# First block of a gated attention kernel: gates in two loads, a reciprocal on VectorE, split hat product, new order of issue

## The chip, the core and the metric

The kernel runs on one core of a Trainium2 chip. A core has a tensor engine (PE, with its weight loads PEld), a vector engine (DVE), a scalar engine for functions by table (ACT), a general engine (POOL) and a sync engine (SP) that mostly issues DMAs; ACT can issue DMAs too, on a queue of its own. Each engine works through its own instructions in the order in which they are written and waits on semaphores for the others. The metric is device time in microseconds of one execution; lower is better.

## The reference

Two stages follow each other. The first is a linear attention with complex gates, over batch 4, 8 heads, 768 tokens and head size 48:

```python
mag = np.sqrt(a_re * a_re + a_im * a_im)
scale = np.minimum(mag, 0.999) / (mag + 1e-06)
a_re_n, a_im_n = (a_re * scale, a_im * scale)
...
for t in range(S):
    new_re = ar * S_re - ai * S_im
    new_im = ar * S_im + ai * S_re
    S_re, S_im = (new_re + kv, new_im)
    y[:, :, t] = np.einsum('bhd,bhde->bhe', q[:, :, t], S_re)
```

`ar`, `ai` are the gates of token t, and `kv` the outer product of its key and value. The second stage is a soft mixture of experts over the 3072 tokens: slot logits, a softmax over tokens that forms 32 slot inputs, eight experts of two layers, and a softmax over slots that combines their outputs.

## The kernel before

The 768 tokens of a batch are 6 blocks of 128; the 4 batches make 24 blocks, each with the 384 values (8 heads of 48) of a token along the free dimension. Three blocks are one unit (u), loaded together: gates into `aat` (real and imaginary part), q and k into `qkt`, values into `vt`, each tile in two buffers. The first unit is loaded in pieces by `load_first`, the first block's pieces by themselves.

The recurrence is turned into products. `gates` makes from a gate its log magnitude and its tangent: Ln of the real part, the reciprocal of the real part as the exponential of minus that Ln, imaginary part times reciprocal, the square with a running maximum, Ln(1 + square), and three more steps that clip the magnitude. Its steps alternate between ACT and DVE. `arctan` gives the phase. `expo` sums log magnitudes over the tokens of a block by one product with a triangle of ones (L731) and takes exp(+) and exp(-) on ACT (L738, L740); the last row of it, the block's decay, goes to DRAM (`rows`, L743) and comes back transposed as `rt` (`decay`, L747). `phase` sums phases in the same way (L696, L700), rounds them (L704) and makes sine and cosine (L714, L719). `mults` multiplies q and k by the exponentials (L754) and then both by cosine and sine into `hat` (L759). `xpose` turns `hat` on PE (L771) and copies it out (`hT`), `score` multiplies and masks (L782, L786), `attend` gives the block's output, and `delta` carries the state on: the product of k's `hat` and v (L820), the sum with the state before (L825) and the decay from `rt` (L827). `xform`, `logits`, `slots` and `shares` feed the second stage, whose expert products come at the end.

Everything runs in an order written by hand as a list, `ORDER`. Each name in it is a task, and each time that it occurs the task goes on by one step; `_InOrder.pin` fixes each engine's sequence to the list. Steps of different engines do not wait for each other because of the list, only because of data or buffers. The names that matter here: `i` a piece of the first loads; `L` and `T` the two loads of ACT's function table; `g0` the gates of the first block, `g1` those of the other two of the first unit, `g2` on those of later units; `t` the arctangent; `e`, `p`, `m` `expo`, `phase` and `mults` of a block; `x` an `xpose` (four a block; odd numbers are k, even ones q), `c` a score, `a` the output, `D` the state; `la`, `lq`, `lv` the loads of a later unit; `d` the return of the decay rows of a unit; `gl` and `rp` smaller loads on SP; `wu` one of 19 filler products on PE with a tile of zeros (L937), whose result nothing reads; `w` a load of expert weights.

The first unit's gates go through `gates` twice, as group 0 (block 0) and group 1 (blocks 1 and 2); the other groups are whole units. In group 0 the working tiles are 128 by 384, in group 1 128 by 768, from group 2 on 128 by 1152.

Of the kernel before, what the change touches and what calls it, by code (L numbers as in the profile page):

```python
# [310 lines left out]


ORDER = """
    i0 wu17 L0 wu5 wu1 g0 g0 g0 g0 g0 g0 g0 i3 g0 i4 g1 g1 i1 tr0 i2 g1 wu7 g1 wu6 la0 e0 e0 e0 wu18 wu9 wu14 T0 t0 e0 m0 p0 p0
    t1 wu13 p0 p0 p0 p0 L1 p1 p1 p1 wu8 m0 rp1 rp1 g1 g1 g1 p2 wu15 wu16 i6 p1 x3 g1 x3 wu10 p2 p2 p2 x2 g2 x2 g2 g2 i7 e1 wu3
    e1 wu4 e2 e2 e2 wu12 gl0 x0 e1 x1 c1 D0 g2 g2 D0 m1 T1 lq0 rp0 t2 x0 x1 c0 p1 p1 wu11 c1 p1 p2 gl1 p2 p2 g2 gl2 p3 p3 L2 g2
    la1 c0 a0 a0 a0 m1 m2 x5 x5 p3 x7 g2 x7 wu2 x4 x4 wu0 p3 m2 e1 e2 d0 D0 i8 g3 g3 g3 g3 e3 e3 e3 m3 e3 e5 e5 x6 e5 x10 x10
    x11 p4 x11 p4 p4 e4 p4 D1 g3 g3 c2 D1 D1 p5 e4 e4 lv0 p5 x6 x8 x9 c3 g3 c2 T2 p3 p3 p3 x8 x9 g3 t3 a1 c3 a1 a1 m3 e4 p5 p4
    p4 D2 D2 m4 p4 p5 p6 D1 p5 p5 c4 D2 D2 p6 c4 p5 x13 p6 la2 c5 x13 e5 d1 c5 m5 D3 x12 g4 a2 rp0 a2 m4 x12 c6 c6 L3 p7 a2 l0
    l0 l0 g4 e6 x19 g4 g4 lq1 e6 x16 e6 x16 e8 p7 e8 e8 g4 p7 p7 p8 x19 D3 D3 lv1 x14 m6 x14 f2 f2 g4 g4 e7 e7 e7 x15 x15 f0 x18  # L320
    x18 x17 x17 q0 q0 q0 f0 D4 D3 g4 p8 s0 m5 p8 e6 D4 q0 c7 c7 c9 la3 x21 T3 e7 t4 x21 g4 a3 a3 w0 x20 s0 c8 p6 p8 p6 c9 p6 q0
    x23 a3 p9 s0 q0 x22 x20 p9 x23 g5 e8 d2 c8 a4 a4 D4 x22 m6 D5 x27 x26 p7 p7 p7 lq2 p8 p8 p8 q0 x27 c10 m7 p9 m7 p9 a4 x26
    e10 p9 c11 L4 g5 c10 x24 x24 g5 f1 f1 p10 e9 e10 e10 D5 x25 x25 c11 D4 a5 a5 x31 x31 m8 m8 g5 e9 g5 e9 e9 c13 c13 a5 g5 x29
    s0 c12 D5 c12 x28 p10 p10 p10 e11 p11 e11 lq3 e11 x29 g5 p9 x28 x33 x33 m9 a6 a6 a6 l1 x30 l1 g5 x30 p11 p11 T4 g5 p11 c14
    c14 D6 m11 D6 D6 p9 x32 x32 p11 p11 l1 f4 f4 x34 t5 q1 x34 D6 c15 p10 f3 p10 p10 x35 p11 x35 f3 D7 D7 la4 p12 c15 e10 a7 g6
    lv2 a7 a7 m9 x36 x36 c16 q1 L5 m10 m10 c16 D7 D7 w1 c17 c17 p12 x37 p12 x37 g6 s0 q1 a8 c18 s0 p13 c18 g6 g6 g5 q1 g6 x41
    x41 p13 p13 p13 g5 a8 a8 x38 x38 x43 x43 x39 x39 D8 p14 q1 e11 s1 d3 x42 x42 x40 q1 q1 g6 g6 a9 e12 e12 e12 f5 e14 e14 e14
    D8 D8 x40 m11 e13 e13 e13 c19 c19 f5 lv3 g6 c21 m12 p14 p14 c20 T5 x45 x45 f6 f6 a9 la5 p14 D9 c21 t6 s1 x46 D9 e12 g6 a9
    p12 p12 p12 p13 g6 c20 x44 s1 p15 D8 p13 p13 f7 D9 f7 p14 p15 p15 x46 x44 x47 x47 e13 l2 a10 a10 m12 x51 x51 w2 g6 g7 p15
    p16 l2 c22 m13 p15 p15 p15 x48 x48 c22 x50 x50 m13 p14 D9 D10 m14 D10 p16 a10 p16 p16 s1 x49 x49 c23 q2 x52 c25 p14 L6 e15  # L330
    c24 e15 g7 e15 q2 q2 e16 m14 g7 a11 c23 a11 e14 d4 a11 D10 D11 x52 c25 p17 l2 s2 x56 g7 c24 g7 e16 e17 x53 x53 e17 e17 D11
    e16 q2 D11 x54 x55 x55 a12 g7 a12 x56 x54 a12 l3 l3 g7 s1 x57 lq4 x57 x58 g7 x58 s1 p17 T6 D12 c26 D12 m15 m15 p17 c27 q2 f8
    c28 t7 p16 p16 c26 p16 q2 c27 e15 p17 p17 f8 x59 x59 g7 q2 e16 x60 p18 p18 a13 gl0 m16 p18 p18 p18 e17 c28 a13 a13 p19 x60
    c29 p17 s2 s2 lq5 p17 la6 g7 p18 D11 x61 f10 lv4 c29 D12 D12 i5 s2 s2 a14 a14 g7 m16 x61 L7 g8 c30 s2 f10 p19 D13 D13 g8 x67
    lv5 x67 d5 c30 p19 x63 x63 x62 q3 x62 f11 f11 x64 m17 m17 x64 D13 f9 x66 w3 a14 x65 x65 p19 p20 c31 c31 q3 g8 l3 f9 a15 a15
    x66 gl1 e18 e18 e18 c32 s3 a15 q3 g8 g8 g8 e20 e20 c33 c33 e20 D14 e19 D14 x70 e18 f12 e19 l4 x70 e19 T7 t8 e19 f12 e20 D13
    c32 a16 q3 a16 a16 m18 x71 x69 x71 x69 m18 x72 x73 g8 l4 p20 w4 x72 p20 x68 x68 p19 D14 D15 D14 p19 p19 m19 x73 p20 p21 D15
    p20 s3 s3 p20 p20 c35 m19 c35 L8 c34 c34 s3 c36 q4 q3 q3 q3 l4 x75 q4 g8 g8 x74 x74 x75 a17 a17 a17 c36 s3 s3 w5 l5 l5 x76
    g8 g8 s4 x76 x77 x77 c37 d6 f13 c37 gl2 e22 e22 e22 m20 p21 m20 a18 a18 x78 f13 c38 p21 l5 D15 f14 x78 lv6 q4 q4 f14 p21 p22
    x79 e23 e23 e23 D16 q4 D16 c38 q4 q4 D16 x80 x80 p22 p22 p22 p23 e21 f15 f15 D17 x79 q5 e21 q5 e21 T8 D16 p21 p21 x82 D17  # L340
    c39 x81 f16 a18 s4 x81 lq6 e21 e22 p21 p23 x82 a19 c39 m22 a19 a19 f16 s4 s4 m21 m21 s4 f17 f17 p22 p23 c40 x83 D17 D18 c40
    x86 p23 x83 p23 p22 x86 x87 x87 p22 s4 c41 c41 a20 p23 p23 a20 x85 D17 x85 L9 x84 x84 f18 w6 w7 a20 D18 w8 m22 x91 x91 m23
    m23 q5 q5 c43 c43 l6 f18 x90 c42 x94 x93 x93 q5 q5 x94 x90 c42 a21 a21 c45 a21 e23 d7 D18 D18 D19 l6 l6 c45 x89 x89 x88 q5
    D19 x88 x92 x92 x95 x95 c44 D19 c44 f20 c46 s5 s5 D19 q6 q6 a22 a22 s6 s5 q6 q6 q6 a22 c46 c47 a23 f20 c47 a23 q6 q6 s5 s5
    s5 a23 l7 w9 f19 f19 w10 l7 l7 s6 s6 s6 q7 q7 f23 me0 me0 f21 q7 q7 s7 s6 s6 f23 ze0 f22 f21 f22 s7 w13 er4 s7 s7 me0 me0
    me0 me0 s7 s7 me0 er4 me0 er0 er1 q7 er1 q7 er0 si0 si0 w12 w11 G0 er2 H0 H0 H0 H0 q7 H0 H0 H0 H0 H0 H0 R0 U0 er2 er7 er8 H0
    er7 U0 U0 H0 R1 X0 X0 X0 X1 X1 er6 U1 X0 X0 X0 G0 U1 U1 X0 X0 X0 X1 X1 er8 er6 X0 X0 X0 X0 X0 X0 w14 w15 G0 G0 X0 O0 O0 X1
    X1 X1 X1 X1 w16 w17 w18 A0 A2 A2 er5 A1 A1 A0 X1 X1 X1 X1 X2 X1 X1 X1 O1 A4 er3 er5 A5 A4 A6 S0 A5 A6 S2 X2 X2 X2 X2 X2 er3
    A3 A3 O1 A8 A8 A7 A7 S3 A9 A10 X2 A9 X2 X2 X2 X2 X2 S1 G0 X2 X2 X2 X2 O2 A11 A11 A10 S5 S4 A12 G0 A13 O2 A14 A12 A13 S6 A15
    A15 A19 A19 A18 A14 S8 A18 S11 S7 A16 A16 A20 A20 S10 A17 A17 S9 G0  # L350
"""


# [192 lines left out]
def _polar(ctx, tc, cst, phi_sb, rp, bad, aa, qk, vv, phi, w1, w2, consts, out):  # L546

    nc = tc.nc
    PE, ACT, DVE, POOL, SP = nc.tensor, nc.scalar, nc.vector, nc.gpsimd, nc.sync
# [51 lines left out]
    def load_first(x):
        if x in (0, 3, 4) and 0 not in aat:
            aat[0] = io.tile([P, UB, 2, HD], F32, name="aat")
        if x in (2, 7) and 0 not in qkt:
# [15 lines left out]
        SP.dma_start(out=o, in_=i)  # L620
# [14 lines left out]
    def gates(x):  # L635
        u, j0, j1 = GROUPS[x]
        ar, ai = aat[u][:, j0:j1, 0], aat[u][:, j0:j1, 1]
        if u not in tmp:
# [5 lines left out]
        ACT.activation(out=ar, in_=ar, func=AF.Ln)
# [1 line left out]
        ACT.activation(out=t, in_=ar, func=AF.Exp, scale=-1.0)  # L646
# [1 line left out]
        DVE.tensor_tensor(out=ai, in0=ai, in1=t, op=ALU.mult)  # L648
# [102 lines left out]
    def mults(g):  # L751
        u, j = divmod(g, UB)
        qk = qkt[u][:, j]
        DVE.tensor_tensor(out=qk, in0=ee[g], in1=qk, op=ALU.mult)  # L754
# [4 lines left out]
        DVE.tensor_tensor(  # L759
            out=x,  # L760
            in0=qk.rearrange("p w (h d) -> p w h d", d=D).unsqueeze(3).broadcast_to(sh),
            in1=cs[g].unsqueeze(1).broadcast_to(sh),
            op=ALU.mult,
        )
# [358 lines left out]
```

## Time and profile before

| | us |
|---|---|
| three runs | 285.72, 286.18, 286.17 |
| median | 286.17 |
| the profiled execution | 285.81 |
| its span, first to last instruction | 283.8 |

All durations here come from one profiled execution, whose span is the time from its first to its last instruction. A row of the order in time gives the start, the duration, the engine, the line of the kernel, the operation, what it writes and reads, the shapes, how many instructions the row merges, and in brackets how long the engine was idle before it and what ended that. An engine's name with a q behind it is its sequencer, which issues DMAs. A row of the stretches gives the length of the stretch and each engine's busy time in it. A row of a tile gives the least, middle and largest duration in ns. Busy time of PE includes the fillers, and starts of neighbouring instructions on one engine can overlap a little.

### The profile page before, as it was taken

The numbers are of one execution on the slowest core, as the hardware profiler recorded it, in microseconds if no ns is written. First come the engines' busy times: TensorE is split into PE (matmuls) and PEld (weight loads), VectorE is DVE, ScalarE is ACT, GpSimd is POOL, SyncE is SP. The second block draws the span as 40 slices with busy tenths as digits, with TensorE's granted clock in tenths as the row PEclk, the third lists the DMA queues.
The fourth block names the chain that finished last, engine by engine and source line by source line (L and its number), as shares of the span: only waits on it lengthen the run. The fifth ranks groups of instructions, "written<-read, shape, count | busy, mean of one in ns | idle before, by whom it ended". The sixth has DMA issues, their size and how long they took to land.

```text
span 283.8 us, 6886 instructions
## 1 busy us (share of the span) xinstructions
PE 272.3 (96%) x2835; PEld 216.4 (76%) x2835; DVE 227.9 (80%) x411; ACT 220.9 (78%) x398; POOL 4.9 (2%) x11
## 2 busy tenths in 40 slices
PE   8999999999999999999999999999999999999970
PEld 3347658979888987989989799988888996438650
DVE  2689998999999999999999999999779566523550
ACT  4776999999999999999999999988886454111250
POOL 0200000000000000000000000000000002000000
PEclk9999999999999999999999999999999999999997
DMA  7996236453653962092457550884068599998395
GB/s 253 392 321 222 66 24 142 155 197 105 212 170 21 338 209 50 38 270 56 163 27 266 181 188 1 60 311 182 3 112 334 193 425 416 420 419 355 126 366 191
DMA packets 21398, 56.61 MB, mean 200 GB/s; under 512 B 11696, under 2 KB 13552, under 8 KB 16496
## 3 DMA queue, kind: packets, MB, share of 16 engines
q1 hardware_dynamic: 20968, 56.10, 59.7%
q8 instruction: 24, 0.39, 0.6%
q14 instruction: 14, 0.11, 0.1%
q10 hardware_dynamic: 392, 0.00, 0.1%
HBM read 51.34 MB, written 4.76 MB: 198 GB/s over the span
## 4 chain that ended last, share of the span: by engine, by line


## 5 line engine op out<-in xcount | busy, mean ns | idle before, releaser
L777 ACT COPY hT<-tp 96x512 f32<-96x512 f32 x92 | 51.2, 588 | 7.3 <-PE tp L771 6.9
L771 PE MATMUL tp<-cst,hat 128*96 128x128 f32 x384 | 53.7, 274 | 0.0
L782 PE MATMUL sp<-hT,hT 96*128 96x128 f32 x384 | 50.9, 278 | 0.0
L782 PEld LDWEIGHTS sp<-hT,hT 96*128 96x128 f32 x384 | 46.9, 192 | 2.0 <-issue 0.7
L771 PEld LDWEIGHTS tp<-cst,hat 128*96 128x96 f32 x384 | 41.8, 128 | 8.3 <-issue 5.2
L759 DVE TENSOR_TENSOR hat<-qkt,cs 128x1536 f32<-128x1536 f32 x24 | 42.0, 1750 | 1.2 <-PE tp L771 0.4
L786 DVE TENSOR_TENSOR scT<-sp,cst 128x512 f32<-128x512 f32 x48 | 32.6, 684 | 6.9 <-PE sp L782 6.8
L807 PE MATMUL yb<-scT,vt 128*48 128x128 f32 x384 | 36.2, 277 | 0.0
L820 PEld LDWEIGHTS db<-vt,hat 128*96 128x96 f32 x320 | 31.0, 165 | 2.5 <-issue 1.5
L820 PE MATMUL db<-vt,hat 128*96 128x48 f32 x320 | 31.5, 245 | 0.0
L809 PE MATMUL yb<-hT,st 96*48 96x128 f32 x320 | 31.1, 272 | 0.0
L807 PEld LDWEIGHTS yb<-scT,vt 128*48 128x48 f32 x384 | 20.7, 122 | 8.1 <-issue 5.1
L754 DVE TENSOR_TENSOR qkt<-ee,qkt 128x768 f32<-128x768 f32 x24 | 22.7, 946 | 0.4 <-ACT ee L740 0.4
L937 PE MATMUL wp<-xs 128*128 128x512 f32 x38 | 21.3, 682 | 1.0 <-POOL xs L932 1.0
L696 PE MATMUL up<-aat,cst 128*128 128x384 f32 x48 | 20.0, 498 | 0.5 <-ACT ee L740 0.2
L809 PEld LDWEIGHTS yb<-hT,st 96*48 96x48 f32 x320 | 19.1, 123 | 0.0
L812 ACT COPY yT<-yb 128x512 f32<-128x512 f32 x24 | 14.2, 591 | 4.8 <-PE yb L809 4.7
L719 ACT ACTIVATE cs<-n,kb 128x384 f32<-128x384 f32 x24 | 14.6, 613 | 0.7 <-DVE n L717 0.7
L648 DVE TENSOR_TENSOR aat<-aat,gt 128x1152 f32<-128x1152 f32 (+2 forms) x9 | 11.0, 1222 | 4.9 <-ACT gt L646 4.9
L832 PE MATMUL xp<-cst,yT 128*128 128x128 f32 x96 | 14.5, 274 | 0.0
L937 PEld LDWEIGHTS wp<-xs 128*128 128x128 f32 x38 | 7.8, 220 | 8.5 <-issue 5.3
L709 DVE SCALAR_TENSOR_TENSOR f<-n,up 128x384 f32<-128x384 f32 x24 | 13.1, 547 | 1.5 <-ACT n L706 1.4
(147 smaller groups left out, 448.3 us busy)
## 6 DMA issues: line engine op xcount, KB each, us to landing
wx<-in_w_dram SPq DMA_DIRECT2D x13, 1024.0 KB
aat<-in_aa_dram SPq DMA_DIRECT2D x7, 1152.0 KB
qkt<-in_qk_dram SPq DMA_DIRECT2D x7, 1152.0 KB
we<-in_w_dram SPq DMA_DIRECT2D x5, 1024.0 KB
vt<-in_vv_dram SPq DMA_DIRECT2D x8, 576.0 KB
aat<-in_w_dram SPq DMA_DIRECT2D x2, 1024.0 KB
qkt<-in_w_dram SPq DMA_DIRECT2D x2, 1024.0 KB
wt<-in_w_dram SPq DMA_DIRECT2D x2, 1024.0 KB
```

Of the source, the lines that this page charges most:

```text
L696: PE.matmul(out=up, lhsT=tri_u[par], rhs=ph, start=True, stop=not by_pe)
L719: ACT.activation(out=t[:, :, 0, :], in_=a.rearrange("p (h d) -> p h d", d=D), func=AF.Sin, scale=-TWO_PI, bias=kb[:, 2:3])
L754: DVE.tensor_tensor(out=qk, in0=ee[g], in1=qk, op=ALU.mult)
L759: DVE.tensor_tensor(out=x, in0=qk.rearrange("p w (h d) -> p w h d", d=D).unsqueeze(3).broadcast_to(sh), in1=cs[g].unsqueeze(1).broadcast_t ...
L771: PE.transpose(out=tp[:, a, :], in_=hat[g][w][:, 4 * hh + a].rearrange("p c d -> p (c d)"), identity=ident)
L777: ACT.copy(out=hT[g, hh, w], in_=tp)
L782: PE.matmul(out=sp[:, a, :], lhsT=hT[g, hh, 1][:, a, :], rhs=hT[g, hh, 0][:, a, :], start=True, stop=True)
L786: DVE.tensor_tensor(out=t, in0=sp, in1=mask[g % 2].unsqueeze(1).broadcast_to([P, 4, P]), op=ALU.mult)
L807: PE.matmul(out=o, lhsT=vt[u][:, j, h, :], rhs=scT[g, hh][:, a, :], start=True, stop=first)
L809: PE.matmul(out=o, lhsT=st[g - 1][:, h, :], rhs=hT[g, hh, 0][:, a, :], start=False, stop=True)
L820: PE.matmul(out=db[:, h, :], lhsT=hat[g][1][:, h].rearrange("p c d -> p (c d)"), rhs=vt[u][:, j, h, :], start=True, stop=True)
L937: PE.matmul(out=wp.rearrange("p (a c) -> p a c", a=4), lhsT=blank, rhs=blank.unsqueeze(1).broadcast_to([P, 4, P]), start=True, stop=True)
```

## The change

Five things change, the first four in the first unit alone.

1. The gates of block 0 come in two loads instead of one: the real part on SP's queue (`i0`), the imaginary part as a new piece `i9`, issued by ACT ahead of its first table load.
2. In group 0 DVE's `reciprocal` takes the place of ACT's exponential of minus Ln. Ln is still needed; it writes over the real part, and comes behind the reciprocal.
3. `mults` of block 0 makes `hat` in two instructions, k's half and then q's, instead of one.
4. The loads of the first unit are issued in another order: the gates of block 2 before those of block 1, and q and k of blocks 1 and 2 (`i7`) before those of block 0 (`i2`).
5. `ORDER` is a new list, over the whole length of the kernel, of the same tasks: other positions of products, copies, loads and fillers on every engine.

On DVE the new list begins with the first block's steps as before; then the two halves of `hat` stand in front of p1's rounding, and D0's multiply with the decay stands in front of m2's `hat`. On PE four fillers instead of five stand in front of e0's product, three behind it as before, and the q transpose x2 stands ahead of the k transpose x3. On SP the sequence begins (list names):

```
before: i0 i3 i4 i1 i2 la1 rp1 i6 i7 gl0 lq1 rp0 gl1 gl2 la2 e1 e2 d0 d0 i8 ...
after:  i0 i4 i3 i1 i7 i2 rp1 la1 i6 i8 e1 la2 e2 d0 d0 lq1 gl1 lq2 la3 lv1 ...
```

The diff, with the list cut to its first lines:

```diff
 ORDER = """
-    i0 wu17 L0 wu5 wu1 g0 g0 g0 g0 g0 g0 g0 i3 g0 i4 g1 g1 i1 tr0 i2 g1 wu7 g1 wu6 la0 e0 e0 e0 wu18 wu9 wu14 T0 t0 e0 m0 p0 p0
-    t1 wu13 p0 p0 p0 p0 L1 p1 p1 p1 wu8 m0 rp1 rp1 g1 g1 g1 p2 wu15 wu16 i6 p1 x3 g1 x3 wu10 p2 p2 p2 x2 g2 x2 g2 g2 i7 e1 wu3
...
+    i9 wu0 wu11 wu4 i0 g0 L0 i4 g0 g0 g0 g0 g0 g0 g0 i3 g1 g1 g1 i1 wu1 e0 e0 e0 i7 i2 wu2 wu12 g1 T0 wu16 tr0 t0 p0 rp1 e0 m0
+    wu10 t1 p1 p0 p0 p1 p0 p0 p0 m0 m0 wu5 L1 p1 g1 g1 p2 wu8 p1 x2 x2 wu9 g1 g1 la0 x3 x3 p2 p2 wu6 p2 x1 x1 e2 g2 g2 i6 D0 g2
...
@@ load_first
-        if x in (0, 3, 4) and 0 not in aat:
+        if x in (0, 3, 4, 9) and 0 not in aat:
...
-            lambda: (aat[0][:, 0:1], aa[0][:, 0:1]),
+            lambda: (aat[0][:, 0:1, 0], aa[0][:, 0:1, 0]),
...
+            lambda: (aat[0][:, 0:1, 1], aa[0][:, 0:1, 1]),
         )[x]()
-        SP.dma_start(out=o, in_=i)
+        (ACT if x == 9 else SP).dma_start(out=o, in_=i)
@@ gates
+        if x < 1:
+            DVE.reciprocal(out=t, in_=ar)
+            yield "g2"
         ACT.activation(out=ar, in_=ar, func=AF.Ln)
-        yield "g2"
-        ACT.activation(out=t, in_=ar, func=AF.Exp, scale=-1.0)
+        if x >= 1:
+            yield "g2"
+            ACT.activation(out=t, in_=ar, func=AF.Exp, scale=-1.0)
         yield "g3"
@@ mults
-        sh = [P, 2, H, 2, D]
-        DVE.tensor_tensor(
-            out=x,
-            in0=qk.rearrange("p w (h d) -> p w h d", d=D).unsqueeze(3).broadcast_to(sh),
-            in1=cs[g].unsqueeze(1).broadcast_to(sh),
-            op=ALU.mult,
-        )
+        for w in (slice(0, 2),) if g else (slice(1, 2), slice(0, 1)):
+            sh = [P, w.stop - w.start, H, 2, D]
+            DVE.tensor_tensor(
+                out=x[:, w],
+                in0=qk[:, w].rearrange("p w (h d) -> p w h d", d=D).unsqueeze(3).broadcast_to(sh),
+                in1=cs[g].unsqueeze(1).broadcast_to(sh),
+                op=ALU.mult,
+            )
+            if w.start:
+                yield "m1"
-    for x in range(9):
+    for x in range(10):
         at("i", load_first, x)
```

More of the change, by code (lines that the diff above doesn't have):

```diff
@@ L322 @@
[L322 to L325, printed above, removed]
@@ new lines @@
+    g3 D1 c2 gl1 lq1 c2 p5 p5 x9 e5 e5 la2 g3 p5 m3 g3 D2 T2 p3 p5 c3 p3 p3 p5 p5 p5 lv0 x10 x10 c3 x11 g3 gl2 m3 t3 rp0 wu13 a1
+    a1 x11 c4 D1 D2 a1 x13 p6 p4 p4 p4 x12 x13 x12 c5 e6 p6 D2 D3 e3 e4 m5 L3 e5 c4 a2 d1 c5 a2 g4 a2 p6 c6 g4 l0 e6 e6 D3 m4 m4
+    D2 e6 g4 x14 x14 p7 p7 l0 c6 p7 l0 s0 x15 x15 D3 g4 g4 p7 x19 x19 e7 e7 e7 x18 x18 D4 D4 g4 f0 f0 x17 m5 e8 e8 e8 q0 q0 q0
+    x16 x16 c7 x17 p8 g4 p8 p8 f2 g4 c7 m6 x23 T3 i5 e7 p6 rp0 f2 p6 p6 p8 x23 c8 a3 q0 c9 q0 m8 q0 a3 a3 x22 c8 x22 t4 x21 x21
@@ new lines @@
+    x20 s0 D3 a4 c9 a4 c11 x20 c10 p8 p8 p8 m6 g4 lv1 x24 D4 a4 la3 q0 g5 D5 p7 D5 p7 p7 L4 g5 gl0 s0 x24 p9 p9 p9 D4 e9 f1 m7
+    f1 g5 c11 c10 w0 e9 e9 a5 a5 m7 x26 e8 d2 D5 D6 x28 x27 x26 a5 lq2 x27 p9 p10 p10 p10 e10 lv2 g5 x28 e10 e10 g5 g5 x25 p10
+    x30 x30 D6 l1 x31 x25 m8 e11 x31 l1 q1 e11 e11 c13 g5 g5 q1 q1 lq3 x29 c12 x29 T4 t5 p11 p9 p9 c13 m10 f3 p11 c12 c14 a6 a6
+    x33 p11 f3 p9 D6 D7 a6 q1 D6 p10 m9 c14 p11 p11 p10 p10 p11 x32 x32 c15 c15 p11 a7 a7 la4 m9 g5 D7 D7 x33 L5 p12 p12 x34 a7
@@ new lines @@
+    p12 D7 x34 s0 c16 e9 e10 c16 m11 q1 q1 g5 x37 x37 x35 x35 s0 s0 q1 g6 a8 e11 D8 d3 g5 x36 x36 D8 c17 g6 l1 s1 m10 e12 g6 e12
+    e12 e12 x39 x39 c17 e14 e14 e14 x38 x38 x40 c18 p13 x40 g6 a8 c18 x41 x41 p13 p13 x43 x43 s1 x42 D8 g6 p13 p14 s1 g6 g6 c19
+    c19 f4 f4 a8 p14 p14 e13 f6 e13 x42 f6 e13 g6 T5 p12 p12 D8 D9 p14 D9 m11 c21 t6 a9 a9 m12 c20 a9 e13 p13 p12 m14 f5 c21 f5
+    l2 x47 x47 la5 x46 e14 c20 x45 x46 D9 p15 p14 g6 x45 p15 p14 p14 lv3 f7 f7 p13 x44 x44 l2 c23 q2 d4 m12 a10 a10 p13 D9 p15
```

54 lines of the change are left out of this document (23 added, 31 removed).

## The prediction

> **What bounds the kernel now.** I read the page first, then the engines' busy time by stretch, then the first 20 us in order of time. The chain of waits that ended last is empty in this trace, so the bound has to be read from who idles where. Engines and, below them, stretches (busy us of PE, its weight loads, DVE, ACT, POOL; granted clock; DMA share; GB/s):
>
> ```profile
> span 283.8 us, 6886 instructions
> PE 272.3 (96%) x2835; PEld 216.4 (76%) x2835; DVE 227.9 (80%) x411; ACT 220.9 (78%) x398; POOL 4.9 (2%) x11
> ```
>
> ```profile
> 0.00:5.00 5.00, 4.01 (x5) 1.85 (x6) 0.66 (x6) 2.12 (x3) 0.41 (x5) 1.00 0.63 217
> 5.00:10.00 5.00, 4.56 (x9) 1.73 (x8) 2.31 (x6) 3.12 (x6) 0.48 (x1) 1.00 1.02 388
> 60.00:80.00 20.00, 20.00 (x197) 17.66 (x196) 19.53 (x32) 19.90 (x40) 0.00 (x0) 1.00 0.42 133
> 160.00:180.00 20.00, 20.00 (x233) 18.48 (x230) 18.89 (x30) 19.85 (x37) 0.00 (x0) 1.00 0.35 88
> 200.00:220.00 20.00, 20.00 (x222) 17.67 (x221) 16.14 (x29) 15.74 (x30) 0.00 (x0) 1.00 0.53 159
> ```
>
> In 60 to 180 ACT is never free (19.9 of 20 us) and DVE hardly (18.9 to 19.5): this middle moves only if it starts earlier or has less to do. From 200 PE has no gap while the others have some. In the first 10 us ACT works 5.2 and DVE 3.0 us, and PE mostly runs the filler products of L937: this stage is latency, one block's gates in a single file. A microsecond gained or lost there moves the start of a full pipeline, and I carry it to the end unless something absorbs it. The file itself:
>
> ```profile
> 4.13 0.52 ACT L644 ACTIVATE aat<-aat 128x384 f32<-128x384 f32 x1 [2.11 <-DMA aat<-in_aa_dram]
> 4.68 0.52 ACT L646 ACTIVATE gt<-aat 128x384 f32<-128x384 f32 x1
> 5.24 0.56 DVE L648 TENSOR_TENSOR aat<-aat,gt 128x384 f32<-128x384 f32 x1 [3.67 <-ACT gt L646]
> 5.83 0.56 DVE L650 CUSTOM_DVE_ANT_0 gt<-aat 128x384 f32<-128x384 f32 x1
> 6.43 0.62 ACT L652 ACTIVATE gt<-gt,kb 128x384 f32<-128x384 f32 x1 [1.23 <-DVE tmax L650]
> 8.32 0.56 DVE L658 SCALAR_TENSOR_TENSOR aat<-aat,gt 128x384 f32<-128x384 f32 x1 [0.68 <-ACT gt L656]
> 8.93 0.91 PE L731 MATMUL lp<-aat,cst 128*128 128x384 f32 x2 [0.44 <-DVE aat L658]
> 9.88 0.49 ACT L738 ACTIVATE ee<-lp 128x384 f32<-128x384 f32 x1
> ```
>
> Gates land at 4.13; Ln and the exponential end at 5.20; the multiply starts at 5.24; each following step starts 0.04 to 0.05 us after the one before it, up to the first product at 8.93.
>
> **The reciprocal.** It replaces the exponential (0.52 us) and takes Ln out of the file: the multiply now waits for the reciprocal alone. Ln writes over the reciprocal's input, so it starts after it, but beside the multiply and the square (5.24 to 6.39 before), whose 1.15 us hide its 0.52. No reciprocal of 384 elements is in the trace; of its kind there are 3 elements and 1:
>
> ```profile
> L150 DVE TENSOR_SCALAR csum<-csum x8: 168/169/169, 69.5 to 239.1; 128x3 f32<-128x3 f32 x8
> L151 DVE RECIPROCAL csum<-csum x8: 175/176/177, 69.7 to 239.3; 128x3 f32<-128x3 f32 x8
> L131 DVE TENSOR_SCALAR nm<-m x1: 150/150/150, 60.0 to 60.0; 96x1 f32<-96x1 f32 x1
> L220 DVE RECIPROCAL rz<-rz x1: 158/158/158, 242.2 to 242.2; 96x1 f32<-96x1 f32 x1
> 9.93 0.96 DVE L648 TENSOR_TENSOR aat<-aat,gt 128x768 f32<-128x768 f32 x1 [1.05 <-ACT gt L646]
> 41.26 0.95 DVE L754 TENSOR_TENSOR qkt<-ee,qkt 128x768 f32<-128x768 f32 x1
> ```
>
> An ordinary DVE operation pays (0.96 - 0.56) / 384 = 1.04 ns an element. **Lower end**: the reciprocal does too, 0.56 us. **Upper end**: the line through its own two rows, (176 - 158) / 2 = 9 ns an element, 0.158 + 383 x 0.009 = 3.6 us. TENSOR_SCALAR makes the same step from 1 to 3 (150 to 169), so the step alone proves nothing. But the reciprocal's own rows are the nearest there are, and I take them, with the smallest slope that they allow, (175 - 158) / 2 = 8.5 ns: **3.4 us**. [...]
>
> **Two loads, two queues.** Before:
>
> ```profile
> 0.73 1.34 SPq L620 DMA_DIRECT2D aat<-in_aa_dram  x3
> 0.73 1.28 ACT L580 ACT_TABLE_LOAD   x1 [0.73 <-PEq L1100]
> 10.40 1.23 ACTq L743 DMA_DIRECT2D rows<-ee  x1
> ```
>
> The real parts, half of the bytes, now come first; the imaginary ones go out on ACT's queue beside them. If a half lands sooner by its share of the transfer, 192 KB at 388 GB/s = 0.5 us, the reciprocal starts at 3.65; if both halves share the engines it starts at 4.1, as before. I take 3.9. [...] Issuing on ACT stands ahead of the table load: SP's three take 1.34 us, 0.45 each; ACT's only one takes 1.23. The load then ends at 2.5 to 3.3, still before 3.9: hidden. Without that cover Ln would pay, which nothing waits for before 8 us.
>
> Sum of the gates: reciprocal 3.9 to 7.3, multiply at 7.33 instead of 5.24: **+2.1 us** (with 0.56 us: multiply at 4.5, -0.75). The first product, ACT's two exponentials, the table load behind them and the phase follow at the same distance; first-block work on ACT is one file, so nothing else fills it. At +2.1 the other loads are not late: the first block's q and k, now behind the 768 KB of the other two, have, by the tiles' shapes, 192 + 192 + 768 + 320 + 768 + 384 KB = 2.69 MB to wait for; 5 x 217 + 5 x 388 GB/s is 3.0 MB by 10 us, against a use after the exponentials of 9.88.
>
> **k ahead of q.** Before, p1's rounding stood in front of the hat product:
>
> ```profile
> 15.20 0.60 ACT L719 ACTIVATE cs<-n,kb 128x384 f32<-128x384 f32 x1
> 15.93 0.56 DVE L704 TENSOR_SCALAR n<-up 128x384 f32<-128x384 f32 x1 [0.80 <-PE up L700]
> 16.41 1.75 DVE L759 TENSOR_TENSOR hat<-qkt,cs 128x1536 f32<-128x1536 f32 x1
> 18.08 0.96 DVE L654 SCALAR_TENSOR_TENSOR aat<-aat,gt 128x768 f32<-128x768 f32 x1
> ```
>
> Now the two halves come right after the cosine and the rounding after them. Each half is L754's form, 0.95 us, and such rows start 0.08 us before the end of the one before: 1.82 for both instead of 1.75, 0.07 more. They save about 0.6 of waiting for the rounding and hand it to the rounding. The new order gives PE a q transpose first (x2 ahead of x3), so k's earlier half serves only the state product D0. Net for the gate of the next blocks (L654, behind both in either order): 0.
>
> **A wait that the new order adds.** DVE's first state multiply (L827) needs the last decay row, which goes through DRAM and back:
>
> ```profile
> 25.06 0.33 SPq L591 DMA_DIRECT2D aat<-in_aa_dram  x1
> 25.50 1.56 SPq L743 DMA_DIRECT2D rows<-ee  x2
> 35.15 0.81 SPq L747 DMA_DIRECT2D rt<-rows  x2
> 36.17 1.75 DVE L759 TENSOR_TENSOR hat<-qkt,cs 128x1536 f32<-128x1536 f32 x1
> 37.84 0.55 DVE L827 TENSOR_TENSOR st<-db,rt 96x384 f32<-96x384 f32 x1
> ```
>
> Rows left at 25.50 to 27.06 and were back only after 35.96. The multiply stood behind m2's hat (36.17 to 37.92) and needn't have waited. It now stands ahead of that hat, so it comes due some 1.75 us earlier in its engine; one of the two rows now goes ahead of the 1152 KB gate load, which brings the return forward by up to about 1 us. The wait is between 0 and 1.75 us; I take 0.9 on DVE, with m2's hat, the next gates and through them ACT queued behind it. ACT has other blocks' work ready, so I count half: +0.4. The same order puts block 3's q and k (lq1) behind that return on SP, and the other loads that share its queue; their users come after 41 us, so 0, between 0 and 1 if the rows come back late. DVE's idle time elsewhere (0.5 to 1.1 of 20 us in the middle) gives 0.4 back.
>
> The rest of the new order is the same set of operations, 19 fillers included; its effect is bounded by ACT's and DVE's idle time in one stretch, 0.1 to 1.1 us, either way, and I take 0.
>
> **Sum**: 2.1 + 0.4 - 0.4 = +2.1 on the profiled execution's 285.81 (283.8 of span and 2.0 around it): 287.9. That execution lies 0.36 below the median of the three runs, so the median should read **288.2**.
>
> **Rivals.**
>
> *The reciprocal at one element a cycle* (ends on the other side). Price 0.56 us; then the multiply starts at 4.5, q's half of the hat ends at 16.9 instead of 18.16, and the next gate's L654 starts about 0.7 us earlier, less 0.4 for the state multiply's wait: -0.5 with a range of -1.3 to +0.3, 285.7 in the median. It decides as soon as the reciprocal costs less than what it replaces with the time won at landing, 5.20 - 3.9 = 1.3 us. For it: the ordinary slope and TENSOR_SCALAR's equal step. Against: its own two rows.
>
> *The clock falls too.* At the end PE's clock dropped once PE had stopped:
>
> ```profile
> 274.48 0.86 PE L301 MATMUL o<-er,sr 128*128 128x512 f32 x3 [0.34 <-ACT os L307]
> 276.60:280.00 3.40, 0.00 (x0) 0.00 (x0) 0.00 (x0) 0.00 (x0) 0.00 (x0) 1.00 0.99 353
> 280.10:283.80 3.70, 0.00 (x0) 0.00 (x0) 0.00 (x0) 0.00 (x0) 0.00 (x0) 0.50 0.11 40
> 0.99 7.50 PE L937 MATMUL wp<-xs 128*128 128x512 f32 x10 [0.99 <-POOL xs L932]
> 13.39 1.02 PE L937 MATMUL wp<-xs 128*128 128x512 f32 x2
> ```
>
> Half clock came between 4.6 and 4.8 us after the last matmul (275.34). The new order has four fillers (8 of the first 10 matmuls, which end at 8.49) ahead of the first product; they end about 1 us sooner, 7.5. With a slow reciprocal the product comes at 11.0, a gap of 3.5 us. That is under 4.6, so I expect no fall; if it falls, the three fillers behind that product take up to twice their 1.02 us each, 3.1 more at most, of which part lies beside ACT's table load: +2.5 on the forecast, 290.7.
>
> *The order costs or gives more than its stretch shows*, the reciprocal being cheap: 286.9, one whole 1.75 us of the state multiply's wait with nothing regained.
>
> **How the numbers follow.** Forecast 0.50 (own range 287.2 to 289.2: the reciprocal from 2.6 to 3.6 us, the wait from 0 to 1.75 with half counted); cheap reciprocal 0.36; clock 0.07; order 0.07. A measurement of this kernel tells about 0.2% (0.6 us) from no change. The cheap reciprocal splits into 0.21 faster, 0.12 the same, 0.03 slower; the order's case into 0.02 faster, 0.03 the same, 0.02 slower; the forecast gives 0.48 slower and 0.02 the same; the clock 0.07 slower. So faster 0.23, same 0.17, slower 0.60. The range that leaves out no more than 2 in 10 runs from the cheap reciprocal's better half to the forecast's end: 285.2 to 289.2.
>
> **What would show it.** Right: a RECIPROCAL of 128x384 at about 3.4 us between 3.9 and 7.3; the first product near 11.0; PE idle from about 7.5; L827's first row with a wait for the rows' return. Wrong: that reciprocal near 0.56 us and the first product near 8.2 (then the time falls); or the late start kept to 25 us but gone by 180, where ACT's busy share would have had to be below the 19.9 of 20 it shows now.

## The result and the profile after

| | before | after |
|---|---|---|
| time, median (runs) | 285.95 us (285.63 to 286.18, 4) | 291.04 us (290.23 to 291.13, 4) |
| profiled execution | 285.81 | 290.96 |
| its span | 283.8 | 289.2 |
| end of the last copy of yT | 235.74 | 239.92 |
| from there to the end of the span | 48.0 | 49.2 |

The change makes the kernel slower: 1.0173 times the time before (95% interval 1.015 to 1.0195), 5.1 us where the prediction had 2.1. The medians below leave out two single runs that were over 1.5% above the fastest of the same kernel, one of e4's six and one of o3's. The profile of the changed kernel, span and engines:

```profile
span 289.2 us, 6879 instructions
PE 273.2 (94%) x2835; PEld 217.6 (75%) x2835; DVE 229.9 (80%) x413; ACT 220.0 (76%) x397; POOL 4.5 (2%) x11
```

Busy time is nearly what it was (DVE has 2.0 us more, with the reciprocal's 2.55 in it). The loss is waiting, and the last copy of yT (the end of the attention part) divides it: 4.2 us are lost ahead of it and 1.2 behind. These are the copy's rows in the two traces (start, us), of the kernel before:

```profile
235.16 0.58 ACT L812 COPY yT<-yb 128x512 f32<-128x512 f32 x1 [2.08 <-PE yb L809]
```

and of the changed kernel:

```profile
239.35 0.57 ACT L821 COPY yT<-yb 128x512 f32<-128x512 f32 x1
```

The beginning of the changed kernel in order of time, DVE and then PE:

```profile
4.16 2.55 DVE L646 RECIPROCAL gt<-aat 128x384 f32<-128x384 f32 x1 [2.59 <-DMA aat<-in_aa_dram]
6.75 0.56 DVE L653 TENSOR_TENSOR aat<-aat,gt 128x384 f32<-128x384 f32 x1
18.55 1.83 DVE L766 TENSOR_TENSOR hat<-qkt,cs 128x768 f32<-128x768 f32 x2 [0.70 <-ACT cs L724]
20.80 0.96 DVE L659 SCALAR_TENSOR_TENSOR aat<-aat,gt 128x768 f32<-128x768 f32 x1
...
0.99 5.22 PE L946 MATMUL wp<-xs 128*128 128x512 f32 x8 [0.99 <-POOL xs L941]
10.44 1.23 PE L736 MATMUL lp<-aat,cst 128*128 128x384 f32 x2 [4.23 <-DVE aat L663]
11.46 4.17 PE L946 MATMUL wp<-xs 128*128 128x512 f32 x6
15.46 0.81 PE L701 MATMUL up<-aat,cst 128*128 128x384 f32 x2
```

The reciprocal takes 2.55 us, so the multiply starts at 6.75 (5.24 before) and the first product at 10.44 (8.93): 1.5 us late. The reciprocal starts on the gates at 4.16, where Ln started at 4.13: in this execution the two loads bring nothing. Then the delay grows. The fillers end at 6.21, PE idled 4.23 us ahead of that product, and the next six matmuls, three fillers, take 4.17 us. The clock in stretches of the same kernel (the third column from the end):

```profile
5.00:10.00 5.00, 1.21 (x3) 0.19 (x1) 3.57 (x6) 1.96 (x4) 0.40 (x1) 1.00 1.04 365
10.00:15.00 5.00, 4.56 (x7) 2.13 (x8) 3.36 (x5) 4.64 (x7) 0.62 (x1) 0.66 0.97 353
10.00:11.00 1.00, 0.56 (x2) 0.43 (x3) 0.39 (x1) 0.97 (x2) 0.00 (x0) 0.96 1.00 283
14.00:15.00 1.00, 1.00 (x3) 0.53 (x2) 0.45 (x1) 1.00 (x2) 0.00 (x0) 0.84 0.88 276
```

Granted 0.66 from 10 to 15, with 0.50 in each stretch of one microsecond from 11 to 14: half speed for about 3.4 of the 5 us. So the first phase product comes at 15.46, and the next blocks' gate (L659) at 20.80 where its counterpart stood at 18.08: 2.7 us late. The state multiply, for which the prediction counted a wait, has none: the copies of its row leave SP at 37.52, and the multiply's own row shows no idle time ahead of it (rows of the changed kernel):

```profile
37.52 0.81 SPq L752 DMA_DIRECT2D rt<-rows  x2
40.10 0.55 DVE L836 TENSOR_TENSOR st<-db,rt 96x384 f32<-96x384 f32 x1
```

### The profile page after: what moved, and what is told of

Its sections match the earlier page's. It is cut to its first block, busy times and chain, and to the rows that moved or that the text cites. A ratio compares the mean times of both kernels' runs of the same rounds, so it can differ in the third digit from the quotient of the medians.

```text
span 289.2 us, 6879 instructions
## 1 busy us (share of the span) xinstructions
PE 273.2 (94%) x2835; PEld 217.6 (75%) x2835; DVE 229.9 (80%) x413; ACT 220.0 (76%) x397; POOL 4.5 (2%) x11
## 4 chain that ended last, share of the span: by engine, by line
PE 91%; DVE 3%; ACT 1%; DMA 1%; issue 1%
PE sp L791 16%; PE tp L780 15%; PE db L829 9%; PE yb L816 9%; PE yb L818 6%; PE up L701 6%; PE wp L946 5%; PE op L272 4%; PE hp L242 4%; PE xp L841 4%; PE lp L736 3%; PE lg L119 3%; PE sip L186 2%; PE o L301 2%; PE lp L739 2%; PE up L705 1%
## 5 line engine op out<-in xcount | busy, mean ns | idle before, releaser
L791 PE MATMUL sp<-hT,hT 96*128 96x128 f32 x384 | 51.5, 279 | 0.0
L766 DVE TENSOR_TENSOR hat<-qkt,cs 128x1536 f32<-128x1536 f32 (+1 forms) x25 | 42.1, 1686 | 1.1 <-ACT cs L724 0.7
L829 PEld LDWEIGHTS db<-vt,hat 128*96 128x96 f32 x320 | 30.4, 165 | 2.3 <-issue 1.8
L719 ACT ACTIVATE cs<-f 128x384 f32<-128x384 f32 x24 | 12.4, 523 | 3.0 <-DVE f L714 3.0
L736 PE MATMUL lp<-aat,cst 128*128 128x384 f32 x24 | 10.4, 514 | 4.2 <-DVE aat L663 4.2
```

Source lines behind the costliest of these rows:

```text
L736: PE.matmul(out=lp, lhsT=mask[par], rhs=aat[u][:, j, 0], start=True, stop=True)
L766: DVE.tensor_tensor(out=x[:, w], in0=qk[:, w].rearrange("p w (h d) -> p w h d", d=D).unsqueeze(3).broadcast_to(sh), in1=cs[g].unsqueeze(1) ...
L791: PE.matmul(out=sp[:, a, :], lhsT=hT[g, hh, 1][:, a, :], rhs=hT[g, hh, 0][:, a, :], start=True, stop=True)
L829: PE.matmul(out=db[:, h, :], lhsT=hat[g][1][:, h].rearrange("p c d -> p (c d)"), rhs=vt[u][:, j, h, :], start=True, stop=True)
```

## The experiments

The runs were made in four groups, each on one chip with the kernel before beside it: e1 to e4 (before: 285.03 us), o1 to o3 and after_again (286.00), o4, o5, p1 and f1 (285.84), o6, o7 and b1 (285.95). "Over" is against the kernel before of the same group. Intervals are 95%.

### Parts of the change at the start: e1 to e4, p1

**e1_exp_back**: the changed kernel with the exponential of before in place of the reciprocal.

```diff
-        if x < 1:
-            DVE.reciprocal(out=t, in_=ar)
-            yield "g2"
         ACT.activation(out=ar, in_=ar, func=AF.Ln)
-        if x >= 1:
-            yield "g2"
-            ACT.activation(out=t, in_=ar, func=AF.Exp, scale=-1.0)
+        yield "g2"
+        ACT.activation(out=t, in_=ar, func=AF.Exp, scale=-1.0)
```

> The changed kernel with the exponential of minus Ln back in block 0; loads, split hat and the new list stay. Theory A (three separate losses: the reciprocal's 2.55 us, a fall of the clock in the gap that it makes, and the new list): the multiply starts near 5.25 instead of 6.75, the first product near 8.95, the gap ahead of it is under 3 us and the clock holds, so -1.5 and -1.3: 288.2 us, still 2 above the kernel before. Theory B (the late start is absorbed in the full middle and the list alone costs): 290 us or more. Theory C (the reciprocal is all): 286.0 us.

290.56 us, 1.018 (1.0162 to 1.0197): 5.5 over. That is the number of Theory B, but no test of it, for this run doesn't isolate the reciprocal. In the new list the first step of g0 stands ahead of L0; with Ln in that place ACT loads two tables one after the other, the second in the middle of the gates:

```profile
1.19 1.28 ACT L645 ACT_TABLE_LOAD   x1 [1.19 <-PEq L1105]
4.45 1.28 ACT L580 ACT_TABLE_LOAD   x1
```

So the multiply comes only 0.45 us earlier than in the changed kernel, and the clock fell here too, after a gap of 2.41 us ahead of the first product (granted 0.66 from 10 to 15 us).

**e2_recip_alone**: the kernel before with nothing but the reciprocal (the first two lines taken out above, put into the old code).

> The kernel before, with its old list, and only the reciprocal in place of the exponential. Theory A: the multiply starts at 6.7, the five fillers of the old list end at 7.0 to 8.5, so the gap ahead of the first product at 10.4 is 2 to 3.4 us and the clock holds: 286.0 + 1.5 = 287.5 us. If the clock falls all the same: up to 289. Theory B: 286.0 to 286.3 us.

286.73 us, 1.0078 (1.0048 to 1.0109): 1.7 over. The six runs fall into two groups: four of 286.05 to 286.83 us at a mean clock of 0.989 to 0.993, 1.4 over in their middle (Theory A had 1.5), and two of 288.64 and 288.84 us at 0.984. The trace is of one of the four, PE, DVE and the last copy on ACT:

```profile
0.99 7.26 PE L941 MATMUL wp<-xs 128*128 128x512 f32 x10 [0.99 <-POOL xs L936]
10.32 0.91 PE L735 MATMUL lp<-aat,cst 128*128 128x384 f32 x2 [2.06 <-DVE aat L662]
11.06 2.74 PE L941 MATMUL wp<-xs 128*128 128x512 f32 x6
...
4.01 2.55 DVE L645 RECIPROCAL gt<-aat 128x384 f32<-128x384 f32 x1 [2.44 <-DMA aat<-in_aa_dram]
...
236.54 0.58 ACT L816 COPY yT<-yb 128x512 f32<-128x512 f32 x1 [2.08 <-PE yb L813]
```

The same 2.55 us; the first product is 1.39 late (10.32 against 8.93) and the last copy of yT still 1.38 (236.54 against 235.16). A delay at the gates is carried through the whole middle undiminished. Five fillers stand ahead of the product here, the clock holds in this execution (granted 1.00 from 10 to 20 us), and the three fillers behind it take 2.74 us. The two slower runs left no trace. One fall of 3.4 us at half speed, as the changed kernel has it, lowers the mean clock of 286 us by 0.006 (half of 3.4, divided by 286), about what these two lack; that the clock fell in them is likely and not shown.

**e3_more_fillers**: the changed kernel with three more fillers ahead of the first product.

```diff
-    ... i1 wu1 e0 e0 e0 ...
+    ... i1 wu1 wu19 wu20 wu21 e0 e0 e0 ...
```

> The changed kernel with three more fillers ahead of the first product, so that PE works until 8.8 to 10.2 us. Theory A: no fall of the clock in 10 to 15 us, the three fillers behind the first product take 2.6 us instead of 4.2, the phase's product starts at about 14.1 instead of 15.5: 291.0 - 1.3 = 289.7 us. Rival (the slow fillers lie beside ACT's table load and hold nothing up): 291.0 us.

289.63 us, 1.0159 (1.0143 to 1.0176): 4.6 over. Theory A and the rival, reckoned on 285.95, had 3.7 and 5.1 over, so the time by itself decides little. The trace does:

```profile
0.99 8.43 PE L946 MATMUL wp<-xs 128*128 128x512 f32 x14 [0.99 <-POOL xs L941]
9.97 0.91 PE L736 MATMUL lp<-aat,cst 128*128 128x384 f32 x2 [0.55 <-DVE aat L663]
10.71 2.74 PE L946 MATMUL wp<-xs 128*128 128x512 f32 x6
13.67 0.91 PE L701 MATMUL up<-aat,cst 128*128 128x384 f32 x2 [0.22 <-ACT aat L689]
...
237.69 0.57 ACT L821 COPY yT<-yb 128x512 f32<-128x512 f32 x1
```

With PE kept busy (0.55 us idle ahead of the first product) the clock holds, 1.00 from 10 to 20 us: 2.74 us for what took 4.17, the phase product 1.8 us earlier, the last copy 1.7 (237.69 against 239.35). Of this 0.5 us is an earlier start: the first product comes at 9.97 here and at 10.44 there, as the gates landed sooner in this execution. So the clock's fall is real and costs about 1.2 us up to the last copy. In the medians it shows less: the changed kernel is 4.8 over in the next group, on another chip, and their intervals overlap; its size lies between 0.2 and 1.2 us. Above all, e3 starts like e2 and is 2.9 us slower: the larger part of the loss is neither reciprocal nor clock.

**e4_no_fillers_p3**: the changed kernel without the fillers wu3, wu18 and wu14, which run together ahead of p3's phase product.

> The changed kernel without the three fillers ahead of p3's product (31.6 to 34.3 us). If they hold p3 up (its arctangent is ready at 32.5), p3's product starts at 32.5, g3's exponential ends some 1.5 us earlier, and the time falls to 289.5 us. Rival (p3 is late anyway, the loss after 35 us comes from the order of copies on ACT): 291.0 us.

289.85 us, 1.0186 (1.0148 to 1.0225): 4.8 over, nothing gained that would show; theory and rival, reckoned on 285.95, had about 3.5 and 5 over. p3's phase product starts at 33.36 instead of 34.26 and ACT's busy time from 35 to 45 us rose from 8.48 to 9.79, so the fillers do hold ACT up. But in this execution the clock stood at half from 9.04 to 15.88 us (worked out from 0.52 and 0.56 in the stretches at its two ends), twice as long as in the changed kernel, which may have taken it back; three stretches of e4:

```profile
9.00:10.00 1.00, 0.00 (x0) 0.00 (x0) 0.56 (x1) 1.00 (x2) 0.00 (x0) 0.52 1.19 441
15.00:16.00 1.00, 1.00 (x3) 0.48 (x2) 0.00 (x0) 0.18 (x1) 0.00 (x0) 0.56 0.09 6
35.00:45.00 10.00, 10.00 (x76) 7.49 (x76) 9.07 (x10) 9.79 (x16) 0.00 (x0) 1.00 0.62 221
```

o4 and o7 settle it on a quieter start.

**p1_loads_split**: the kernel before, its list and its exponential, with only the two loads (i9 first) and the two halves of hat.

> The kernel before, its list and its exponential, with only the two loads on two queues (i9 first) and the first block's hat in two halves, k's ahead of q's. Theory (both are hidden: the gates land within 0.3 us of 3.9 us, and the two halves took 1.83 us where one took 1.75): within 0.4 us of the kernel before. Rival (they gain what the forecast gave back, 0.4 us, or more): 0.5 to 1 us less than it.

285.88 us against 285.84, 0.9999 (0.999 to 1.0008), as the theory had it. Loads on two queues and k ahead of q are worth nothing either way under the old list.

### The order by itself: o1 to o3 and after_again

**o1_order_alone**: the code before with the new list. `i9`, `L0` and the second `m0` of that list follow the old code, and `wu2` is moved so that five fillers stand ahead of e0's product; against the list of the changed kernel, shortened:

```diff
-    i9 wu0 wu11 wu4 i0 g0 L0 i4 ... i1 wu1 e0 e0 e0 i7 i2 wu2 wu12 ... m0 m0 wu5 ...
+    wu0 wu11 wu4 i0 L0 g0 i4 ... i1 wu1 wu2 e0 e0 e0 i7 i2 wu12 ... m0 wu5 ...
```

> The kernel before with nothing but the new order of issue: gates in one load (i9 left out), Ln and Exp for the first block with L0 ahead of g0, hat in one multiplication, and wu2 moved ahead of e0 so that five fillers stand there as before and the clock holds. Theory (the new order costs by itself, in small waits of ACT and in the tail): the changed kernel with a held clock (e3, 289.63) stood 2.9 us over the reciprocal alone (e2, 286.73), so 287.7 to 288.7 us where the kernel before has 285.0. Rival (the order costs only when it starts late, as the new list was planned for other durations): 285.0 to 285.6.

288.52 us, 1.0087 (1.0067 to 1.0107): 2.5 over, where the theory, reckoned on 285.0, had 2.7 to 3.7 and the rival 0 to 0.6. This is with the exponential, a clock that holds at the start of its trace (granted 1.00 up to 40 us) and the first product in time (8.80). The order is the largest single part of the loss. The first place where it loses, PE and then ACT:

```profile
28.76 2.81 PE L937 MATMUL wp<-xs 128*128 128x512 f32 x6
31.41 0.81 PE L696 MATMUL up<-aat,cst 128*128 128x384 f32 x2
...
34.62 0.58 ACT L777 COPY hT<-tp 96x512 f32<-96x512 f32 x1 [0.54 <-PE tp L771]
36.16 0.58 ACT L706 ACTIVATE n<-up,kb 128x384 f32<-128x384 f32 x1 [0.96 <-PE up L700]
236.51 0.57 ACT L812 COPY yT<-yb 128x512 f32<-128x512 f32 x1
```

Six filler matmuls in one stretch hold back p3's phase product; everything behind it in PE's queue is late, and ACT, which has no other time to spare, waits 0.54 and 0.96 us. The last copy ends 1.35 us late; from there to the end of the span it takes 49.6 us instead of 48.0.

**o2_new_tail**: the old list up to the third a23, then what is left in the new order.

> The kernel before, its own list up to the third a23, and what is left after that (203 entries) in the order of the new list. From the end of the last yT copy to the end of the span the traces show 48.0 us before, 49.2 in the changed kernel, 49.6 in e3 and 47.1 in e2. Theory (the tail of the new order, with all of H ahead of the turn, loses about half of what the order costs): 286.2 to 287.4 us. Rival (the tail costs nothing by itself): 284.8 to 285.4.

287.64 us, 1.0063 (1.0047 to 1.0079): 1.6 over. The theory, reckoned on 285.0, had 1.2 to 2.4 over.

**o3_new_head**: o1's list up to T2, then what is left in the old order.

> The kernel before, with the list of o1 up to T2 (171 entries, the first 45 us or so) and everything left in the old order. ACT idled 0.9 us more there in e3 than in e2 beyond the same start (0.65+1.51 against 1.51+0.17 us from 25 to 45 us, and 0.4 us each in stages after). Theory (the head loses some tenths, because products and rounding are issued ahead of what ACT needs): 285.4 to 286.4 us. Rival (the head is neutral and all of the loss lies behind it): 284.8 to 285.3.

289.58 us, 1.0115 (1.0089 to 1.0142): 3.6 over, outside both expectations. It tells nothing of the head, for a new loss arose where the two orders meet:

```profile
45.00:60.00 15.00, 13.36 (x122) 11.19 (x122) 13.47 (x18) 13.12 (x21) 0.51 (x1) 0.91 0.64 210
```

ACT is busy 13.12 of 15 us there and 18.52 of the next 20 (14.68 and 19.61 in o1), and the clock fell (granted 0.91 from 45 to 60 us). This list, half of one and half of the other, is worse than either.

**after_again**: the changed kernel on this chip.

> The changed kernel, unaltered, on the chip of these runs, as the mark for o1 to o3 and for e3: 289.7 to 291.0 us. If e3 (289.63) gained from its held clock, this stands 0.8 to 1.4 us above e3; if the clock's fall costs nothing, it equals e3.

290.80 us, 1.0178 (1.015 to 1.0206): 4.8 over, as expected. Its trace has the fall of the clock again, from 10.96 on (granted 0.98 from 10 to 11 us, 0.50 from 11 to 14), and the last copy of yT at 239.33. The comparison stands under e3.

### Where in the order: o4 to o7, f1, b1

**o4_order_less3**: o1 without wu3, wu18 and wu14.

> o1 (the new order alone, 2.5 us over the kernel before) without the fillers wu3, wu18 and wu14, which in its trace run in one stretch of six from 28.76 to 31.57 us, ahead of the phase product of p3; after that ACT waits 0.54 and 0.96 us for TensorE. Theory (that stretch holds up the phase product and with it ACT): the loss falls by 1.0 to 1.5 us, to 1.0 to 1.5 us over the kernel before (287.0 to 287.5 where that has 286.0). Rival (the products behind them wait for something else, or TensorE falls short and the clock with it): 2.3 to 3 us over it, as o1.

287.75 us, 1.0057 (1.0037 to 1.0076). The middle of the six runs says little, for they fall into two groups: 286.97, 286.98 and 287.22 us at a mean clock of 0.989 to 0.990 (1.1 to 1.4 over, as the theory had it), and 288.29, 288.34 and 288.50 at 0.979 to 0.985 (2.5 to 2.7 over). The trace, one of the second group, in order of time:

```profile
30.12 0.91 PE L696 MATMUL up<-aat,cst 128*128 128x384 f32 x2 [0.79 <-ACT aat L684]
```

and in stretches of one microsecond:

```profile
32.00:33.00 1.00, 1.00 (x8) 1.00 (x8) 1.00 (x2) 1.00 (x1) 0.00 (x0) 0.72 0.93 396
33.00:34.00 1.00, 1.00 (x7) 0.96 (x7) 0.97 (x3) 0.99 (x2) 0.00 (x0) 0.50 0.59 192
34.00:35.00 1.00, 1.00 (x3) 0.31 (x2) 0.93 (x2) 0.94 (x2) 0.00 (x0) 0.50 0.17 28
35.00:36.00 1.00, 1.00 (x2) 0.50 (x2) 0.86 (x1) 0.00 (x0) 0.00 (x0) 0.58 0.02 0
```

The phase product is 1.3 us earlier than in o1, but PE idled 0.79 us ahead of it and the clock went to half 2.3 us after it began (0.72 in the stretch from 32 to 33 puts that at 32.44). ACT then waits 1.66 us for the product of L700, 0.70 more than in o1.

**o7_order_less2**: o1 without wu18 and wu14; wu3 stays.

> o1 without wu18 and wu14; wu3 stays. Without all three (o4) the phase product began 1.3 us earlier than in o1, but TensorE idled 0.79 us ahead of it (29.33 to 30.12) and the clock stood at half from 32.3 to 35.6 us; three of its six runs took 287.0 to 287.2 us and three 288.3 to 288.5. Theory (one filler of 0.94 us fills that gap, so the clock holds in every run and the phase product still comes 1.2 us earlier than in o1): 1.0 to 1.5 us over the kernel before. Rival (the gap isn't what lowers the clock, or the stretch isn't what holds up ACT): 1.9 us over it or more, or runs of two kinds again.

287.46 us (286.98 to 288.03), 1.0052 (1.0036 to 1.0069): 1.5 over, 1.0 less than o1 and at the end of what the theory had, with no second group. Its trace:

```profile
28.77 1.09 PE L937 MATMUL wp<-xs 128*128 128x512 f32 x2
29.73 0.91 PE L696 MATMUL up<-aat,cst 128*128 128x384 f32 x2
...
235.52 0.57 ACT L812 COPY yT<-yb 128x512 f32<-128x512 f32 x1
```

One filler bridges the gap, three overfill it, and ACT's two waits of o1 are gone. The last copy is 0.99 us earlier than in o1 and 0.36 later than before: the two fillers were most of what the order lost ahead of it.

**o5_late_tail**: the old list up to the first A; the last 88 entries in the new order.

> The kernel before with its own list up to the first A (1196 entries), and the last 88 entries (combining, the output's copies, the stores) in the order of the new list. In o2 the hidden products, the turn and the experts' products end within 0.2 us of the kernel before (272.35 against 272.17), but the first combining product starts 2.0 us later (264.22 against 262.19) and the last one ends 1.2 later. Theory (the tail's loss lies in the order of combining and stores): 1.2 to 2.0 us over the kernel before. Rival (it lies ahead of them, in the order of the hidden products and the turn): within 0.4 us of it.

288.21 us, 1.0092 (1.0068 to 1.0116): 2.4 over, a little more than the theory's 2.0 at most, and nothing but the last 88 entries differs. The last products and the stores, in the kernel before:

```profile
272.10 0.79 PE L301 MATMUL o<-er,sr 128*128 128x384 f32 x3
273.06 1.08 PE L301 MATMUL o<-er,sr 128*128 128x512 f32 x4 [0.18 <-DVE sr L285]
...
264.90 12.53 SPq L990 DMA_DIRECT2D out_dram<-os  x12
```

and in o5:

```profile
272.47 0.84 PE L301 MATMUL o<-er,sr 128*128 128x384 f32 x3
273.81 1.02 PE L301 MATMUL o<-er,sr 128*128 128x384 f32 x4 [0.51 <-DVE sr L285]
275.01 0.86 PE L301 MATMUL o<-er,sr 128*128 128x384 f32 x3 [0.18 <-ACT os L307]
276.22 0.47 PE L301 MATMUL o<-er,sr 128*128 128x512 f32 x1 [0.35 <-DVE os L309]
...
266.34 13.75 SPq L990 DMA_DIRECT2D out_dram<-os  x12
```

and stretches of o5:

```profile
274.00:276.00 2.00, 1.69 (x7) 0.94 (x6) 1.88 (x4) 0.90 (x2) 0.00 (x0) 1.00 0.72 279
278.00:280.00 2.00, 0.00 (x0) 0.00 (x0) 0.00 (x0) 0.00 (x0) 0.00 (x0) 1.00 0.85 311
```

One combining product more is left for the end, behind a chain of copies that free its accumulators, so PE ends at 276.69 and not at 275.34. The first store is issued at 266.34 instead of 264.90 and the last is done issuing at 280.09 instead of 277.43. The DMA share from 274 to 280 us is 0.72 to 0.85, where the kernel before has 0.93 to 1.05 in the same stretches, and more of the stores is left for the time behind 280.

**o6_tail_asap**: o5 with each store just behind the last copy that it needs.

> o5 (the kernel before with the last 88 entries in the new order, 2.4 us over it) with each store moved to just behind the last copy that it needs; products, copies and their order stay. In o5 the twelve stores are issued from 266.3 to 279.7 us where the kernel before has 264.9 to 276.8, and the list has S2, S3 and S6 four to twelve entries behind their copies. Theory (SP's order of the stores loses, an early piece stands behind a late one): 0.5 us over the kernel before or less. Rival (the order of combining loses, the pieces themselves are ready late): 1.8 to 2.4 us over it.

287.34 us, 1.0054 (1.0033 to 1.0076): 1.4 over, between the two expectations. Of the tail's 2.4 us the order of the stores makes about 1.0 and the order of combining about 1.4; this is rough, for o5 and o6 ran on two chips and their intervals overlap a little.

**b1_stores_asap**: the same move on the kernel before, as an attempt to beat it.

> The kernel before with nothing but its stores moved to just behind the last copy that each needs (S0, S3, S1, S4 and S7 come earlier in SP's queue). The DMA share is 0.51 and 0.67 from 266 to 270 us before, so stores have room there. If the time of the tail is set by when stores are issued: 0.3 to 1.0 us less than the kernel before. If it is set by the last pieces: within 0.2 us of it.

286.46 us, 1.0024 (1.0014 to 1.0035): slower by 0.5, outside both expectations. The trace shows more DMA work up to 270 us (share 0.50 instead of 0.45 from 264 to 270) and less behind it, 0.80 instead of 0.95 from 270 to 276; which store the queue then waited for wasn't followed. As early as possible isn't a rule for stores; this list had them better.

**f1_mended**: the changed kernel with e3's fillers, without wu3, wu18 and wu14, and with the old order from the third a23 on.

> The changed kernel with the named losses of its order taken out: three more fillers ahead of e0 (the clock holds), wu3, wu18 and wu14 left out, and from the third a23 on the old order. What is left of the change is the reciprocal, the loads, the halves and the rest of the new order. Theory (the losses add up and the reciprocal's 1.4 to 1.7 us is what remains): 1.2 to 2.0 us over the kernel before. Rival (the rest of the new order loses as well): 2.5 us over it or more.

287.74 us, 1.0085 (1.0055 to 1.0115): 1.9 over, within what the theory had: the reciprocal's 1.7 of e2 and little else, as far as intervals of this width tell. No version here beats the kernel before.

## Why the prediction went wrong

- **Direction**: right, slower. **Size**: 288.2 against 291.0, outside the range.
- **The step that failed** is "The rest of the new order ... its effect is bounded by ACT's and DVE's idle time in one stretch, 0.1 to 1.1 us, either way, and I take 0." By o1 the order costs 2.5 us. The bound looked at the wrong thing: idle time that the old order has says how little could be won, not how much another order can lose. In a middle where ACT is busy 19.9 of 20 us, every wait that a new order puts in front of ACT is a loss. And it didn't look behind 200 us, where stores and combining set the end and where about half of the order's loss lies (o1: 1.35 us ahead of the last yT copy's end, 1.6 behind it; o2, o5). The two places are shown: a stretch of fillers (o7: 1.0 us), and the last 88 entries (2.4 us in o5; all that lies behind the last yT copy costs 1.2 in the changed kernel's own trace).
- **The reciprocal**: right in mechanism, too large: 2.55 us where 3.4 was taken; its multiply 1.5 us late where 2.1 was forecast. By e2 this alone is 1.7 us (1.4 to 3.1 by the interval), 1.4 in the runs of the higher clock. That the delay is carried to the end unabsorbed was right.
- **The clock**: the rival had the right condition and the wrong verdict. It was refused because the gap was to be 3.5 us, and half clock had come 4.6 us after the last matmul at the end of the kernel. The fillers ended at 6.21, not 7.5, so the gap was 4.23, and the clock fell at 10.92 (worked out from 0.96 in the stretch from 10 to 11), 4.7 after them. That agrees with the 4.6 by luck: the clock fell in e4 2.06 us after the last filler, with PE still idle, in e1 after a gap of 2.41 us, and in o4 after one of 0.79, so a gap of 3.5 us was no safety. The last section has what the traces show of the condition. Cost, 0.2 to 1.2 us by e3, below the 2.5 named; if the clock is what divides e2's two groups, it cost 2.3 there.
- **The state multiply's wait, +0.4, and -0.4 regained**: the wait did not come, and no run shows the 0.4 regained; that they cancelled in the sum was luck.
- **Loads and halves**: worth nothing (p1), as taken for the halves. The 0.2 us that the sum had for an earlier landing can't be seen: with two loads the first step on the gates starts at 3.68 (e3) to 4.16, with one at 3.92 (o1) to 4.25 (o2).
- **Two small sums** are off and decide nothing: the bounds named for the forecast's own range give 287.0 to 288.9 and not 287.2 to 289.2, and 0.7 less 0.4 is not the 0.5 of the cheap reciprocal.

The parts add up. To the end of the last yT copy, in single traces and corrected for starts that differ by 0.1 to 0.5 us: reciprocal 1.5 (e2), clock 1.2 (changed kernel less e3), two fillers 1.0 (o1 less o7), rest of the order 0.5 (o7 less before), together the 4.2 seen; behind it 1.2, in all 5.4 of span. What the rest of the order consists of wasn't tried. The 1.2 is the least certain: the time from that copy to the end is 47.1 to 48.2 us in the traces with the old order there (before, e2, o3, p1, f1) and 48.7 (e4) to 50.4 (o5) with the new one.

## What to carry to other kernels

A new order of issue is a change of its own, to be priced by itself: look for what stands in front of a product that the full engine needs, and for the place of the last stores, and don't bound its loss by the idle time of the old order. Filler products have two sides: too few ahead of a wait and the clock can fall (granted 0.66 from 10 to 15 us in the changed kernel, 1.00 in e3 with three more), too many and the next product is late (31.41 us in o1, 29.73 in o7 with two fewer); count them against the gap that they are to cover. A single trace doesn't tell whether the clock holds in the next execution: look at the spread of the runs and at their mean clock (o4: 286.97 us at 0.989 to 288.50 at 0.979). An operation moved to an idle engine helps only if it is quicker than the whole detour that it replaces: here 2.55 us on DVE against 1.04 for two steps on ACT.
